# Row scaling and logits of the first expert network kept on chip, its iteration spread out, and the first routing's list product with its operands exchanged

## The chip, the cores and the metric

The kernel runs on one core of a Trainium2 chip. The metric is the device time in microseconds (us) of one execution, as a median of several. The engines are TensorE (PE: matmuls; PEld: its weight loads), VectorE (DVE), ScalarE (ACT), GpSimd (POOL, which here clears buffers and issues indirect DMAs) and SyncE (SP, which issues plain DMAs). Each engine works through its own queue in order.

## The reference

```python
def reference(x, moe, moe2):              # x: 8 x 3072 x 256
    h = real(fft(fft(x, axis=1), axis=2)).reshape(24576, 256)
    # first network: 8 experts, 256 -> 1024 -> 256
    P = exp(h @ moe.w_gate - max)
    for _ in range(8):                    # "scaling"
        P /= P.sum(1) + 1e-9
        P /= P.sum(0) + 1e-9
        P *= N / E
    out = sum(P[:, e:e+1] * (relu(h @ moe.w1[e]) @ moe.w2[e]) for e in range(8))
    # second network: 8 experts, each row goes to its best one
    logits = out @ moe2.w_gate
    e = argmax(logits, axis=1); p = softmax(logits)[e]
    return p * (relu(out @ moe2.w1[e]) @ moe2.w2[e])
```

## The kernel before

The program has five stages: the transform (0 to 195 us), a first routing (195 to 245), the first network (245 to 440), a second routing (436 to 470) and the second network (470 to the end). All but a small part of P is negligible, so the first network, too, computes only chosen rows per expert: three tiles of 128 rows for each of the eight experts, and five overflow tiles f0 to f4, whose rows belong to different experts and whose weights are therefore gathered row by row. P has 29 x 8 = 232 columns on 128 partitions. All matrix products of the networks are done in three passes with each operand split in a high and a low part (`w1h`, `w1l`, `xh`, `xl`, `hh`, `hl`, `w2h`, `w2l`); ACT makes the high parts (L831, L857, L887), DVE the low ones (L837, L427, L436).

**First routing.** DVE forms one-hot factors `ah` (128 wide) and `bv` (58 columns: two values of 29 tiles); 64 small matmuls (L560) add their products to a list `pt` of 128 x 58, from which DVE reads row indices (`hidx`), signs and prices; POOL then gathers the rows of the first tiles (`Xg<-H`), DVE puts them together into `x`, PE transposes them (L854) and the first expert's products (L901) start. Around the list product stand gate products (L1264, halves of 16 matmuls that make w2 times the second gate, so that the second network's logits come with the rows) and empty matmuls on zeros (L1283). `G2` is the string that says how many of each (g and w) stand at each of the stage's points.

**First network.** The order of the work is written by hand. A clock of numbered slots runs through the experts: 0 to 20 in each expert, 0 to 7 the first product, 12 to 20 the second product of its three tiles; (e, i) is slot i of expert e. `STEPS` says at which slots, counted from `SINK`, the 18 half turns of the iteration (scaling) are done: a start, matmuls that add up the columns (L1007), a turn on DVE between them, and an end that writes the row weights `Rwt`. Before the end is reached (`known`), the rows y of finished tiles are kept unscaled in buffers (`keep`); after it they are scaled and written to `acc` in DRAM at one or two per slot (`sink`), and tiles that come later are scaled as they leave PSUM (L1649). `SENDS` says at which slots POOL adds the third tile of each expert to `acc` by an indirect DMA, since its rows also belong to another expert. The gathers of an overflow tile's weights (`fw`, `rawc`, `gd`) stand in the same POOL queue.

**Second routing.** It needs the eight logits of each row, which it reads back from `acc` (`ask`); the rows of third tiles are corrected by one matmul with a one-hot matrix (`arrive`, L1408). Then come the argmax, the positions, and a gather of the second network's rows (`Xg<-acc`, L803). `part("u", 0, i)` splits one of the four weight pieces of the second network's first expert.

Of the kernel before, what the change touches and what calls it, by code (L numbers as in the profile page):

```python
# [7 lines left out]
F32 = mybir.dt.float32  # L8
# [554 lines left out]

def route1(nc, rt, L, rmx, K, R, keep, pool, ring, hooks):
# [109 lines left out]
    o.tt(eq, ja[:, NSL:NSL + 8, None].to_broadcast([128, 8, NSL]), ja[:, None, :NSL].to_broadcast([128, 8, NSL]), ALU.is_equal)  # L674
    o.tt(eq, eq, gp[:, None, :NSL].to_broadcast([128, 8, NSL]), ALU.mult)
    hooks[4]()
# [11 lines left out]
    def signs():  # L688
# [9 lines left out]

        o.red(gq, eq, ALU.add)
# [16 lines left out]
    def targets():  # L716

        lq = S([2, E], name="lq")
# [6 lines left out]
        o.cp(R["l7"], lq[:, :, E - 1])  # L725
# [310 lines left out]
def dense(tc, ctx, A, K, rt, R, Ld, H, Pd, out, wg2):  # L1036
# [69 lines left out]
    with tc.For_i(0, NT, 1) as i:  # L1106
# [17 lines left out]
        for s in range(2):  # L1124
# [27 lines left out]
         ("t", 6, "c"), ("t", 7, "a"), ("w1", 1, "a"), ("w2", 1, "b")]  # L1152
# [5 lines left out]
def run(tc, ctx, A, out, H, acc, Ld, Pd, Gd, Zd):  # L1158
# [19 lines left out]
    for nm, sh, dt in (("gm", [1], F32), ("ovf", [1], F32), ("sel", [max(NF1, NF2), 8], F32), ("hidx", [NT1], I32),  # L1178
                       ("sg", [NT1], F32), ("valid", [NT1], F32), ("prim", [NT1], F32), ("apos", [E], I32), ("oidx", [NF1], I32), ("l7", [2], F32),
# [41 lines left out]
    with tc.manual_schedule():  # L1221
# [27 lines left out]
        with ExitStack() as st:  # L1249
# [7 lines left out]
            def gates2(e, qs=(0, 1)):  # L1257
# [16 lines left out]
                if e < 3 or e == E - 1:  # L1274
                    fetch()
# [24 lines left out]
            with ExitStack() as s1:  # L1300
# [39 lines left out]
                def low(k):  # L1340
                    for f in lows[k]:
                        f()

                signs, later = route1(nc, rt, L, rmx, K, R, S, r1, ring, [fill(i) for i in range(1, 5)] + [lambda: low(0)])
# [20 lines left out]
            with ExitStack() as s1:  # L1365
# [4 lines left out]
                def rest():  # L1370
                    later[2]()
                    sp.close()
                    return P(st, "yb", 15, side="right"), P(s1, "sk", 1, side="right")

                lg = kp.tile([128, NT1, 8], F32, name="lg")

                def ask():
# [7 lines left out]
                turned, more = moe1(nc, K, R, acc, moe, W, part, X, xg, Gd, *rows("w1", "w2"), xb, pt, zeros, zt, later[:2] + (rest, lambda: low(1), grab), ask, rt.C("tro"), lambda i: warm(2), lambda: xg.tile([128, CAP, HW], F32, name="Xg").rearrange("p a b -> p (a b)")[:8, :512])  # L1385
            with ExitStack() as s1:
# [8 lines left out]
                def arrive(choose):  # L1395
                    a, b, n8 = E * CAP - CAP, E * CAP, [128, NT1, 8]
                    hot = xg.tile([128, CAP, HW], F32, name="Xg").rearrange("p a b -> p (a b)")
                    oht, ohr, mv = hot[:, :NT1], hot[:, 32:160], hot[:, 160:160 + 8 * NT1].rearrange("p (t e) -> p t e", e=8)
                    o.ts(oht, rt.C("at"), R["l7"][:, 0:1], ALU.is_equal)
                    o.ts(ohr, rt.C("i128"), R["l7"][:, 1:2], ALU.is_equal)  # L1400
# [4 lines left out]
                    o.tt(mv, oht[:, :, None].to_broadcast(n8), lg[:, a:a + 1].to_broadcast(n8), ALU.mult)  # L1405
                    more(Y2[1])
                    p = pt.tile([128, 512], F32, name="pt")
                    nc.tensor.matmul(p[:, :8 * NT1], ohr, mv.rearrange("p t e -> p (t e)"), start=True, stop=True)  # L1408
# [20 lines left out]
                for i in (2, 3):  # L1429
                    part("u", 0, i, nc.vector)  # L1430
# [404 lines left out]
```

## Time and profile before

| | us |
|---|---|
| timed, median of 3 | 666.21 |
| timed, lowest and highest | 665.62, 670.52 |
| profiled execution, its own time | 660.63 |
| span of the profiled execution | 658.5 |
| PE busy in the span | 624.5 |
| DVE, ACT, POOL busy | 430.6, 327.6, 200.5 |

The profiled execution is 5.58 us shorter than the timed median. Differences are worked out against the profiled execution and then taken off the median. "Busy" counts matmuls that overlap with their neighbours; PEclk is the mean clock granted to TensorE, where 1.00 stands for 2.4 GHz and 0.50 for 1.2 GHz.

### The profile page before, as it was taken

The page shows a single profiled execution, that of the slowest core. Times are in us where ns is not written, and L with a number is a line of the kernel's source. Part 1 is how long each engine was busy: PE and PEld are TensorE (multiplying, and loading weights), DVE is VectorE, ACT ScalarE, POOL GpSimd, SP SyncE. Part 2 cuts the span into 40 slices and gives each one's busy share as a digit, 9 for nine tenths or more (in the row PEclk, how much of TensorE's full clock was granted, in tenths as well). Part 3 has the DMA queues.
Part 4 walks back from the last instruction along what each step waited for, and adds up shares of the span by engine and source line. Part 5 has one row for each costly group of instructions (what it writes and reads, how often), then busy time and mean ns, then how long its engine had stood idle before and what let it go on. Part 6 is the DMA issues. An engine that isn't in the chain of part 4 may idle for free.

```text
span 658.5 us, 12591 instructions
## 1 busy us (share of the span) xinstructions
PE 624.5 (95%) x4776; PEld 601.2 (91%) x4782; DVE 430.6 (65%) x958; ACT 327.6 (50%) x731; POOL 200.5 (30%) x326
## 2 busy tenths in 40 slices
PE   9999999999998999997989898999699999999995
PEld 6899999999998988997989798987599999999995
DVE  4697787778238959759899473657345844844751
ACT  3455545555544404755545773652245644744651
POOL 0002220122010078850101142201486665322342
PEclk9999999999999869998999898999799999999998
DMA  8999999999989865876747897787465367347321
GB/s 220 293 235 298 272 262 285 274 278 305 353 266 347 352 191 172 235 254 201 248 135 231 275 241 264 182 262 246 150 226 190 127 235 299 116 194 272 133 117 36
DMA packets 60142, 152.66 MB, mean 232 GB/s; under 512 B 11651, under 2 KB 29195, under 8 KB 52524
## 3 DMA queue, kind: packets, MB, share of 16 engines
q1 hardware_dynamic: 50716, 114.66, 56.6%
q0 software_dynamic: 8896, 36.64, 16.8%
q8 instruction: 39, 0.64, 0.4%
q10 hardware_dynamic: 464, 0.51, 0.2%
q14 instruction: 27, 0.22, 0.1%
HBM read 101.61 MB, written 50.07 MB: 230 GB/s over the span
## 4 chain that ended last, share of the span: by engine, by line
PE 47%; DMA 10%; DVE 8%; ACT 3%; issue 2%; SPq 0%; POOL 0%; POOLq 0%; DVEq 0%; ACTq 0%
PE py L934 19%; PE ph L901 15%; PE ph L947 5%; PE py L1264 3%; DMA out_dram<-zt 2%; DMA acc<-y 2%; DVE hl L436 2%; DMA rawc<-in_w_dram,Rfrow 2%; DVE w2l L837 2%; PE pt L854 1%; PE py L1283 1%; DMA acc<-zt 1%; DMA Xg<-acc,Rgidx 1%; DVE w1l L837 1%; DMA acc<-y,Rapos 1%
## 5 line engine op out<-in xcount | busy, mean ns | idle before, releaser
L934 PE MATMUL py<-w2h,hh 128*128 128x256 f32 (+1 forms) x472 | 137.3, 291 | 0.0
L436 DVE SCALAR_TENSOR_TENSOR hl<-ph,hh 128x384 fp32r<-128x384 f32 (+1 forms) x161 | 84.7, 542 | 79.0 <-ACT hh L887 78.5
L934 PE MATMUL py<-w2h,hl 128*128 128x256 f32 (+1 forms) x472 | 134.9, 286 | 1.2 <-DVE hl L436 1.2
L934 PE MATMUL py<-w2l,hh 128*128 128x256 f32 (+1 forms) x472 | 134.5, 285 | 0.3 <-DVE w2l L839 0.3
L887 ACT ACTIVATE hh<-ph 128x384 fp32r<-128x384 f32 (+1 forms) x161 | 75.7, 482 | 54.7 <-PE ph L901 34.2
L934 PEld LDWEIGHTS py<-w2h,hl 128*128 128x128 f32 x472 | 90.1, 191 | 2.1 <-DVE hl L436 2.1
L934 PEld LDWEIGHTS py<-w2l,hh 128*128 128x128 f32 x472 | 90.3, 191 | 0.5 <-DVE w2l L839 0.5
L934 PEld LDWEIGHTS py<-w2h,hh 128*128 128x128 f32 x472 | 90.3, 191 | 0.1
L901 PE MATMUL ph<-xh,w1h 128*128 128x384 f32 x256 | 68.5, 348 | 3.5 <-DVE hl L436 3.4
L901 PE MATMUL ph<-xl,w1h 128*128 128x384 f32 x256 | 66.3, 340 | 0.0
L901 PE MATMUL ph<-xh,w1l 128*128 128x384 f32 x256 | 66.2, 340 | 0.0
L808 POOL DMA_INDIRECT out_dram<-y,Rorow x30 | 35.1, 1171 | 81.8 <-ACT hh L887 45.8
L126 POOL TENSOR_TENSOR lc<-hd 128x32 f32<-128x32 f32 (+1 forms) x25 | 9.5, 380 | 165.9 <-ACT hd L122 150.8
L74 PE MATMUL pp<-ca,w 96*128 96x96 f32 x512 | 59.0, 275 | 0.0
L74 PEld LDWEIGHTS pp<-ca,w 96*128 96x128 f32 x512 | 58.2, 192 | 0.5 <-ACT Z L97 0.2
L901 PEld LDWEIGHTS ph<-xh,w1h 128*128 128x128 f32 x256 | 45.5, 190 | 6.5 <-DVE hl L436 5.0
L84 DVE COPY t<-pp 128x512 f32<-128x512 f32 (+2 forms) x56 | 33.3, 608 | 24.7 <-PE pp L82 24.7
L91 PE MATMUL pp<-cb,t 128*128 128x128 f32 x368 | 47.5, 276 | 0.6 <-DVE t L84 0.6
L901 PEld LDWEIGHTS ph<-xl,w1h 128*128 128x128 f32 x256 | 47.0, 190 | 0.1
L901 PEld LDWEIGHTS ph<-xh,w1l 128*128 128x128 f32 x256 | 46.9, 189 | 0.0
L76 ACT ACTIVATE at<-pp 128x384 f32<-128x384 f32 x64 | 31.1, 491 | 30.6 <-PE pp L74 30.0
L91 PEld LDWEIGHTS pp<-cb,t 128*128 128x128 f32 x368 | 44.4, 192 | 0.9 <-DVE t L84 0.8
(340 smaller groups left out, 1249.6 us busy)
## 6 DMA issues: line engine op xcount, KB each, us to landing
out_dram<-zt SPq DMA_DIRECT2D x48, 512.0 KB, 6.9
H<-hd SPq DMA_DIRECT2D x24, 562.0 KB, 10.6
xa<-in_xa_dram SPq DMA_DIRECT2D x32, 384.0 KB, 10.5
xm<-in_xm_dram SPq DMA_DIRECT2D x32, 384.0 KB, 8.5
rawa<-in_w_dram SPq DMA_DIRECT2D x8, 1024.0 KB, 5.1
rawb<-in_w_dram SPq DMA_DIRECT2D x8, 1024.0 KB
rawa<-in_u_dram SPq DMA_DIRECT2D x8, 1024.0 KB, 9.9
rawb<-in_u_dram SPq DMA_DIRECT2D x8, 1024.0 KB
```

What stands on the lines that cost most here:

```text
L74: nc.tensor.matmul(p[:M, i], lhs(4 * h + i), ca, start=True, stop=True)
L76: nc.scalar.activation(out=at[:M, :, :, s0:s0 + 4], in_=p[:M].rearrange("m s g j -> m g j s"), func=AF.Copy)
L84: nc.vector.tensor_copy(out=t[:, :n, :M], in_=p[:, :n, :M])
L91: nc.tensor.matmul(p[:M, i * 128:(i + 1) * 128], t[:, i, :M], cb[:, (g0 + i) * 128:(g0 + i + 1) * 128], start=True, stop=True)
L436: self.nc.vector.scalar_tensor_tensor(out, a, s, b, op0, op1)
L808: nc.gpsimd.indirect_dma_start(out=dst, out_offset=bass.IndirectOffsetOnAxis(ap=idx, axis=0), in_=src, in_offset=None, **kw)
L837: eng.tensor_tensor(out=lv, in0=rv, in1=hv.bitcast(F32), op=ALU.subtract)
L887: self.nc.scalar.activation(out=a[:, :n], in_=p[:, :n], func=AF.Relu)
L901: self.nc.tensor.matmul(p[:, :N], w, xx, start=(i == 0), stop=(i == 5))
L934: self.nc.tensor.matmul(p[:, :nd], c, W[2 + m // 4][w][:, m % 4, :nd], start=(m == 0 and i == 0), stop=(m == 7 and i == 2))
L947: self.nc.tensor.matmul(p[:, m * 128:(m + 1) * 128], w[:, k, (m0 + m) * 128:(m0 + m + 1) * 128], x[:, k, i * 128:(i + 1) * 128], start=(k ...
L1264: nc.tensor.matmul(p[:, i * 96:(i + 1) * 96], raw["t", e][k][:, m * 128:(m + 1) * 128], wg2[:, k], start=(k == 0), stop=(k == 1))
```

## The change

It does four things.

1. In the first routing the list product has its operands exchanged: `bv` (58 columns) is now the stationary operand and `ah` (128 columns) the moving one; the result of 58 x 128 is copied by ACT and transposed back by PE (`turned`). A seventh gate half is done ahead of the counts, eight empty matmuls instead of two stand before the product and two gate halves instead of three behind it. Two operations on `eq` and one low part of w1 move behind the reading of the list. The gate weights of expert 7 come into another buffer.
2. The turns of the scaling are spread from 43 to 64 slots: the start moves from slot (2, 8) to (2, 11), the end from (4, 8) to (5, 8). Three more y buffers lie in an `Xg` tile, and the sends begin in expert 5 instead of 4.
3. The scaling of kept rows moves from ACT to DVE; DVE also copies each tile's eight logits to `lg`, and a one-hot pair for each third tile is made there (`spot`). The two DMAs of `ask` that read the logits back are gone; `arrive` does seven matmuls in place of one.
4. `part("u", 0, 3)`, with the fetch that follows it, moves from before the second routing's gathers to slot (0, 1) of the second network.

```diff
+    def swapped(self, pl, ah, bv, a, n, first, last):
+        nv = bv.shape[1] * bv.shape[2]
+        for i in range(n):
+            self.nc.tensor.matmul(pl[:nv, :128], bv[:, :, :, a + i], ah[:, :, i],
+                                  start=first and i == 0, stop=last and i == n - 1)
+
+    def turned(self, pl, nv, t):
+        self.nc.scalar.activation(out=t[:nv], in_=pl[:nv, :128], func=AF.Copy)
+        p = self.pt.tile([128, 512], F32, name="pt")
+        self.nc.tensor.transpose(p[:, :nv], t[:nv], self.K["ident"][:nv, :nv])
+        return p
...
-        rt.put(pl, ah, bv, a, n, a == NSL, a + n == NSL)
+        rt.swapped(pl, ah, bv, a, n, a == NSL, a + n == NSL)
         a += n
+    hooks[4]()
+    pl = rt.turned(pl, 2 * NT1, T([128], name="lt"))
...
-                if e < 3 or e == E - 1:
+                if e < 4:
                     fetch()
...
-                    for a, b in ((0, E * CAP - CAP), (E * CAP, NT1)):
-                        r = row_tile(a) * 128
-                        nc.sync.dma_start(out=lg[:, a:b], in_=acc[r:r + (b - a) * 128].rearrange("(t p) c -> p t c", p=128)[:, :, D:DG])
...
+                    def add(i):
+                        r, m, _ = hot[i]
+                        nc.tensor.matmul(p[:, :8 * NT1], r, m, start=(i == 0), stop=(i == E - 2))
+
                     more(Y2[0])
+                    for i in range(E - 2):
+                        add(i)
                     pg = turned()
...
-                for i in (2, 3):
-                    part("u", 0, i, nc.vector)
+                part("u", 0, 2, nc.vector)
...
+YB = 15
 SINK = (2, 8)
-STEPS = [0, 1, 6, 6, 11, 11, 16, 16, 21, 21, 26, 26, 31, 31, 36, 36, 41, 42]
-FIRST = 3
-ADDS, SENDS = tuple(range(21)), {4: (15, 20), 5: (4, 9, 14, 19), 6: (13, 17), 7: (2,)}
+STEPS = [3, 4, 10, 10, 17, 17, 23, 24, 32, 32, 39, 39, 48, 48, 55, 55, 62, 63]
+FIRST = 1
+ADDS, SENDS = tuple(range(21)), {5: (14, 19), 6: (3, 8, 12, 16), 7: (1,)}
...
-G2 = ("gg", "", "gggggg", "0lz12g3gg", "ggww", "ggg")
+G2 = ("gg", "", "ggggggg", "0lz12g3gg", "ggwwwwwwww", "gg")
...
             if k is None:
-                nc.scalar.activation(out=y[:, :DG], in_=y[:, :DG], func=AF.Copy, scale=R["wt"][:, t:t + 1])
+                o.ts(y[:, :DG], y[:, :DG], R["wt"][:, t:t + 1], ALU.mult)
+            if t // CAP != E - 1:
+                o.cp(lg[:, t], y[:, D:DG])
+                if t < E * CAP and not alone(t):
+                    spot(t // CAP)
+                    hot[-1][2]()
...
+        o.ts(t, rt.C("at"), R["lq"][:, 0, e:e + 1], ALU.is_equal)
+        o.ts(r, rt.C("i128"), R["lq"][:, 1, e:e + 1], ALU.is_equal)
...
+    sl.at(0, 1, lambda: part("u", 0, 3, V))
```

On DVE the place is the end of the scaling. In the kernel before, `Rwt` is the row weights, `xl` and `w1l`, `w2l` the low parts that PE waits for next:

```order
L427 TENSOR_TENSOR pr<-P,Rsel 128x40
L442 TENSOR_REDUCE Rwt<-pr 128x5
L436 SCALAR_TENSOR_TENSOR Rwt<-P 128x24
L427 TENSOR_TENSOR xl<-pt,xh 128x384 x2
L837 TENSOR_TENSOR w1l<-rawa,w1h 128x1024
L837 TENSOR_TENSOR w2l<-rawc,w2h 128x4x256
```

In the changed kernel (where `y` is a tile's rows and `lg` the logits on chip; helper lines stand 13 to 15 further down) the same place reads:

```order
L442 TENSOR_REDUCE Rwt<-pr 128x5
L436 SCALAR_TENSOR_TENSOR Rwt<-P 128x24
L431 TENSOR_SCALAR y<-y,Rwt 128x264
L439 COPY lg<-y 128x8
L431 TENSOR_SCALAR y<-y,Rwt 128x264
L439 COPY lg<-y 128x8
L431 TENSOR_SCALAR y<-y,Rwt 128x264
L439 COPY lg<-y 128x8
L427 TENSOR_TENSOR xl<-pt,xh 128x384 x2
```

Three scalings and their copies now stand between the row weights and `xl`, and more of them between the low parts that follow.

On POOL the place is experts 4 and 5. Before, the additions to `acc` of the third tiles of experts 0 to 3 (by `Rapos`) are mixed with the gathers of overflow tile 4's weights:

```order
L808 DMA acc_58<-y_3445,Rapos_86 1152x265
L808 DMA acc_58<-y_3812,Rapos_86 1536x265
L803 DMA fw_4657<-in_w1_dram,Rfrow_90 128x2048
L808 DMA acc_58<-y_4155,Rapos_86 1920x265
L803 DMA rawc_4716<-in_w2_dram,Rfrow_90 128x2048
L803 DMA gd_4718<-Gd_61,Rfrow_90 128x64
L808 DMA acc_58<-y_4502,Rapos_86 2304x265
```

In the changed kernel:

```order
L816 DMA fw_4629<-in_w1_dram,Rfrow_90 128x2048
L816 DMA rawc_4686<-in_w2_dram,Rfrow_90 128x2048
L816 DMA gd_4688<-Gd_61,Rfrow_90 128x64
L1667 MEMSET y_4835 128x1
L821 DMA acc_58<-y_3461,Rapos_86 1152x265
L821 DMA acc_58<-y_3817,Rapos_86 1536x265
```

All three gathers stand ahead of the first addition to `acc` now; what follows them is the clearing of a column of a y buffer.

## Rows read from the trace of the kernel before

**Rows 1.** What PE waits for from 195 us on: total, times, longest.

```profile
PE pt L1007 <- DVE xl L427: 6.3, 2, 3.8
PE pt L854 <- DMA Xg<-acc,Rgidx: 5.6, 1, 5.6
PE ph L901 <- DVE hl L436: 3.4, 3, 2.6
PE pt L881 <- DVE xl L427: 3.0, 1, 3.0
```

**Rows 2.** Windows, experts 2 to 6: length, busy by engine (PE to POOL), clock, DMA.

```profile
285.60:316.50 30.90, 26.66 (x187) 26.13 (x187) 25.55 (x65) 17.86 (x43) 4.37 (x8) 0.94 0.70 224
316.50:344.40 27.90, 25.39 (x192) 25.18 (x191) 24.76 (x61) 15.13 (x37) 2.94 (x4) 1.00 0.51 169
344.40:375.00 30.60, 27.25 (x192) 26.41 (x191) 22.05 (x51) 20.75 (x50) 4.81 (x5) 0.94 0.78 246
375.00:399.20 24.20, 24.20 (x184) 24.20 (x183) 14.11 (x30) 13.20 (x31) 7.98 (x6) 1.00 0.97 281
399.20:427.90 28.70, 26.08 (x185) 25.76 (x184) 16.82 (x28) 16.43 (x37) 7.68 (x8) 0.94 0.71 199
```

**Rows 3.** The same view, the stretch after the longest of these waits.

```profile
309.20:312.50 3.30, 3.30 (x17) 3.30 (x16) 3.16 (x10) 1.46 (x5) 0.00 (x0) 0.50 0.43 42
```

**Rows 4.** Timeline of DVE in expert 2: start, length, what.

```profile
303.53 0.30 DVE L431 TENSOR_SCALAR P<-P,Rgm 128x232 f32<-128x232 f32 x1
...
307.54 0.56 DVE L442 TENSOR_REDUCE cs<-P 128x8 f32<-128x232 f32 x1
...
310.96 0.16 DVE L433 TENSOR_SCALAR cs<-total 128x8 f32<-128x8 f32 x1
...
313.86 1.21 DVE L837 TENSOR_TENSOR w2l<-rawc,w2h 128x1024 fp32r<-128x1024 f32 x1
```

**Rows 5.** Timelines of ACT, SP, POOL; in brackets idle time before, and its end.

```profile
363.49 2.14 ACT L1657 ACTIVATE y<-y,Rwt 128x264 f32<-128x264 f32 x5 [4.54 <-DVE Rwt L442]
...
401.98 1.06 ACT L831 ACTIVATE w2h<-rawc 128x1024 fp32r<-128x1024 f32 x1 [7.84 <-DMA rawc<-in_w_dram,Rfrow]
...
364.03 0.81 SPq L1669 DMA_DIRECT2D acc<-y  x2
...
366.29 0.10 POOL L1646 MEMSET y<- 128x1 f32 x1 [14.43 <-DMA acc<-y]
...
389.74 1.28 POOL L803 DMA_INDIRECT rawc<-in_w_dram,Rfrow  x1 [0.30 <-issue]
```

**Rows 6.** Timeline of PE in the first routing.

```profile
224.35 0.59 PE L1283 MATMUL py<-zb 128*128 128x512 bf16 x2 [0.36 <-ACT g L1266]
224.99 6.98 PE L560 MATMUL pt<-bv,ah 128*128 128x58 bf16 x64
...
241.92 1.76 PE L560 MATMUL py<-bq,ah 128*128 128x16 bf16 x24
243.53 0.42 PE L854 MATMUL pt<-ident,x 128*128 128x128 f32 x2
...
245.72 0.44 PE L901 MATMUL ph<-xh,w1h 128*128 128x384 f32 x1
```

**Rows 7.** Timeline of DVE there: the last piece of the first tile's rows.

```profile
240.16 0.49 DVE L1602 TENSOR_TENSOR x<-Xg 128x127 f32<-128x127 f32 x2
```

**Rows 8.** The chain that ended last, second routing: start, length, what.

```profile
442.83 0.41 PE pt L1408 x2
...
457.88 1.23 DVE w2l L837
459.33 6.46 DMA Xg<-acc,Rgidx
```

**Rows 9.** Tile Xg in the first routing, 232 to 241 us: its gathers.

```profile
DMA to landing us min/median/max: 2.8/3.0/3.9
```

**Rows 10.** DMA issues, 361 to 400 us: KB each, median us to landing.

```profile
acc<-y SPq DMA_DIRECT2D x5, 132.0 KB, 7.3
```

More of the change, by code (lines that the diff above doesn't have):

```diff
@@ L1342, in low @@
                         f()
-                signs, later = route1(nc, rt, L, rmx, K, R, S, r1, ring, [fill(i) for i in range(1, 5)] + [lambda: low(0)])
+                    lows[k].clear()
+                signs, later = route1(nc, rt, L, rmx, K, R, S, r1, ring, [fill(i) for i in range(1, 5)] + [lambda: lows[0].pop(0)()])
                 X = {}
@@ L1372, in rest @@
                     sp.close()
-                    return P(st, "yb", 15, side="right"), P(s1, "sk", 1, side="right")
+                    return P(st, "yb", YB, side="right"), P(s1, "sk", 1, side="right")
                 lg = kp.tile([128, NT1, 8], F32, name="lg")
+                hot = []
                 def ask():
-                    for a, b in ((0, E * CAP - CAP), (E * CAP, NT1)):
-                        r = row_tile(a) * 128
-                        nc.sync.dma_start(out=lg[:, a:b], in_=acc[r:r + (b - a) * 128].rearrange("(t p) c -> p t c", p=128)[:, :, D:DG])
                     for _ in range(5):
                         zeros(2)
-                turned, more = moe1(nc, K, R, acc, moe, W, part, X, xg, Gd, *rows("w1", "w2"), xb, pt, zeros, zt, later[:2] + (rest, lambda: low(1), grab), ask, rt.C("tro"), lambda i: warm(2), lambda: xg.tile([128, CAP, HW], F32, name="Xg").rearrange("p a b -> p (a b)")[:8, :512])
+                turned, more = moe1(nc, K, R, rt, lg, hot, acc, moe, W, part, X, xg, Gd, *rows("w1", "w2"), xb, pt, zeros, zt, later[:2] + (rest, low, grab), ask, rt.C("tro"), lambda i: warm(2), lambda: xg.tile([128, CAP, HW], F32, name="Xg").rearrange("p a b -> p (a b)")[:8, :512])
             with ExitStack() as s1:
@@ L1404, in arrive @@
                          R["wt"][:, a:b, None].to_broadcast([128, CAP, 8]), ALU.mult)
-                    o.tt(mv, oht[:, :, None].to_broadcast(n8), lg[:, a:a + 1].to_broadcast(n8), ALU.mult)
+                    hot[-1][2]()
                     more(Y2[1])
-                    p = pt.tile([128, 512], F32, name="pt")
-                    nc.tensor.matmul(p[:, :8 * NT1], ohr, mv.rearrange("p t e -> p (t e)"), start=True, stop=True)
+                    add(E - 2)
                     o.tt(lg, lg, p[:, :8 * NT1].rearrange("p (t e) -> p t e", e=8), ALU.add)
@@ L1590, in first, with moe1 @@
         return self.moe.free_first(self.w[f, 0], self.x[f // CAP], f % CAP)
-def moe1(nc, K, R, acc, moe, W, part, X, xg, Gd, w1f, w2f, xb, pt, zeros, zt, rest, ask, trash, warm, grow):
+def moe1(nc, K, R, rt, lg, hot, acc, moe, W, part, X, xg, Gd, w1f, w2f, xb, pt, zeros, zt, rest, ask, trash, warm, grow):
     o = Ops(nc)
@@ L1643, in keep @@
     def keep(t, p):
-        y = late["y"].tile([128, DW], F32, name="y")
+        n = late["n"] = late.get("n", -1) + 1
+        if YB <= n < YB + CAP:
+            if n == YB:
+                late["x"] = xg.tile([128, CAP, HW], F32, name="Xg")
+            y = late["x"][:, n - YB, :DW]
+        else:
+            y = late["y"].tile([128, DW], F32, name="y")
         if t < E * CAP and not alone(t):
@@ L1656, in add @@
             if k is None:
-                nc.scalar.activation(out=y[:, :DG], in_=y[:, :DG], func=AF.Copy, scale=R["wt"][:, t:t + 1])
+                o.ts(y[:, :DG], y[:, :DG], R["wt"][:, t:t + 1], ALU.mult)
[3 more added lines that the diff above has]
+                    spot(t // CAP)
+                    hot[-1][2]()
             if t < E * CAP:
@@ L1677, in send, with spot, moved @@
             scatter(nc, a, i, y, compute_op=ALU.add)
+    def spot(e):
+        if e % 2 or e == E - 1:
+            late["hot"] = xg.tile([128, CAP, HW], F32, name="Xg").rearrange("p a b -> p (a b)")
+        t, r, m = (late["hot"][:, 400 * (1 - e % 2) + a:400 * (1 - e % 2) + b] for a, b in ((0, NT1), (32, 160), (160, 160 + 8 * NT1)))
+        o.ts(t, rt.C("at"), R["lq"][:, 0, e:e + 1], ALU.is_equal)
+        o.ts(r, rt.C("i128"), R["lq"][:, 1, e:e + 1], ALU.is_equal)
+        def moved():
+            n8 = [128, NT1, 8]
+            o.tt(m.rearrange("p (t e) -> p t e", e=8), t[:, :, None].to_broadcast(n8), lg[:, CAP * e:CAP * e + 1].to_broadcast(n8), ALU.mult)
+        hot.append((r, m, moved))
     def begin():
@@ L1687, in moe1 @@
             f()
+    rest[3](0)
     xt = moe.turn(lambda i: x[0][:, i], warm)
-    for i, f in zip((0, 1, 3, 4), (rest[3], rest[0], rest[1], begin)):
+    for i, f in zip((0, 1, 3, 4), (lambda: rest[3](1), rest[0], rest[1], begin)):
         sl.at(0, i, f)
@@ L1733, in moe1 @@
     late["q"] = nc.scalar
+    spot(E - 1)
     def more(n):
```

19 lines of the change are left out of this document (7 added, 12 removed).

## The prediction

> **What bounds the kernel now.** PE is busy for 624.5 of 658.5 us, so the time to be had is where PE waits or runs at half clock. I read first what PE waits for from the first routing on [rows 1]: the scaling's column sums (L1007, 6.3 us in two waits of 3.8 and 2.5), the gather of the second network's rows (5.6), the low part `hl` in the first product (3.4, of which 2.6 in one piece), and the transposes that wait for `xl` (L881, 3.0). Then the windows of experts 2 to 6 [rows 2]. Expert 5 has no wait and takes 24.2 us; the five together take 30.9 + 27.9 + 30.6 + 24.2 + 28.7 = 142.3, which is 21.3 more than five times 24.2. The waits of 3.8, 2.5, 3.0 and 2.6 explain 11.9 of that. After the first of them PE stays busy for 3.3 us with a granted clock of 0.50, 1.2 in place of 2.4 GHz [rows 3]; experts 4 and 6 have the same mean clock of 0.94 as expert 2, while expert 3, whose wait was 2.5 us, has 1.00. Three such stretches of about 3.4 us lose some 1.7 us each, 5.1 in all. So 17.0 us are lost to waits and clock in these experts; the other 4.3 I take for work that differs between them.
>
> **The change part by part.** *Scaling, start and turns.* The start and the first half turn hold DVE from 303.53 to 308.10, 4.6 us, and a later turn from 310.96 to 313.86, 2.9 us [rows 4]. In expert 2 DVE is busy for 25.55 us, in expert 3 for 24.76 [rows 2], both more than the 24.2 in which PE could be done: DVE is the bound there, and the turns are its surplus. Spread from 43 to 64 slots, a pair of turns comes every 7 or 8 slots and not every 5; a slot is 24.2 / 21 = 1.15 us. Expert 2 gives up about one turn (25.55 - 2.9 = 22.7), expert 3 as well (21.9); both then fit under 24.2. The start keeps its 4.6 us and its first product one slot later. I count two slots, 2.3 us, as what PE has in hand, and keep a wait of 2.5 us out of 3.8; for all other turns in experts 2 to 4 I keep 1 us out of the second wait of 2.5.
>
> *Scaling, the end and the scaled rows.* At the end ACT stood idle for 4.54 us until `Rwt` was there and then scaled five tiles in 2.14 us, while what makes `xh` and so `xl` queued behind it [rows 5]: this is the wait of 3.0. Now DVE scales. The nearest price is a DVE operation on 232 columns, 0.30 [rows 4]; with 264 columns and a copy of eight logits I take 0.45 per tile (an estimate from that row; ACT's 2.14 / 5 = 0.43 for the scaling alone would make it 0.6), and 0.7 for a one-hot pair with its product (three operations of 0.2 to 0.3). What is late next is twofold. `xl` now stands behind three scalings and copies on DVE, 1.35 us. And ACT's next kept row needs a y buffer that is freed only when a write to `acc` has landed: before, a write issued at 364.03 released POOL at 366.29, 2.3 us later [rows 5]. With the end of the turn (1.4) and two scalings ahead of it, ACT is blocked for some 4.5 us, and queued behind it are the high parts of the next tile; most of that PE covers with the 24 matmuls of a tile, and I keep 1.2 us of the wait of 3.0. Over expert 5 as a whole DVE gets 14.1 (its own work) + 4.4 (one and a half turns) + 13 x 0.45 = 5.9 + 3 x 0.7 = 2.1, together 26.5 against 24.2: 2.3 us too much, a wait that was not there. Expert 6 comes to 16.8 + 5 = 22 and fits; I put 0.5 there.
>
> *The gathers of overflow tile 4.* In expert 6 ACT waited 7.84 us for `rawc`, whose gather POOL issued only at 389.74, behind additions to `acc` that wait for writes [rows 5]; PE's wait of 2.6 for `hl` and the half clock after it (1.7) follow from that. Now the three gathers stand ahead of all additions, and the additions queue behind them, which nobody in expert 5 or 6 waits for. I take these 4.3 us as gained.
>
> So of the 17.0 us lost there remain 2.5 + 1 + 1.2 + 2.3 + 0.5, and 1 for a half-clock stretch that still occurs: 8.5. **Gain 8.5**, between 17.0 (no wait left) and about 0 (DVE's new work makes as many waits as go).
>
> *The list product.* 64 matmuls take 6.98 us, 109 ns each; the product with 16 moving columns runs at 1.76 / 24 = 73 ns [rows 6]. If the time follows the moving columns, (109 - 73) / 42 = 0.86 ns a column, 128 columns give 169 ns and 10.8 us; if the 73 ns are the floor and the moving columns don't count, 4.7 us. The count of instructions is unchanged and no row shows 58 stationary columns, so I take the 109 ns as they are, between both ends. Six more empty matmuls at 0.3 each, less a little that was spent waiting anyway, start it 1.1 us later; the copy by ACT and the transpose back add 0.9. The list, complete at 224.99 + 6.98 = 231.97, would so be complete at 233.97. From there to the end of the first rows' last piece it was 240.65 - 231.97 = 8.68 us [rows 7], which gives 242.65; PE, which came to the transposes at 243.53 because gate products were in front, now has a half less behind the list and reaches them before that. With 245.72 - 243.53 = 2.2 us from there to the first product [rows 6] it starts at 244.85, **0.9 us earlier**; with 169 ns it is 2.9 later, with 73 ns 3.2 earlier. The two operations on `eq` and the low part of w1 (1.2 like that of w2 [rows 4]) move behind the reading, where DVE waits for the gather; if that didn't hide them they would cost some 2 us, inside these ends. The seventh gate half ahead of the counts is moved, not added: PE waits for DVE there, and without that wait it costs ahead of the list what it saves behind it.
>
> On this product the Trainium skill speaks on both sides. "TensorE: Matmul & The Clock Gate", section "Weight-path perf modes — Fast Weight Load (FWL) and DoubleRow", says that weights are read fast only when there are 128 of them, which 58 stationary columns would give up; its section "Back-to-back issue gap" has 81 ns for a matmul with 128 moving columns, by which the product would be 5.2 us and this term about 2.7. The trace agrees with neither yet, since its 109 ns stand at 58 moving columns.
>
> *The second routing.* `arrive` gets six more matmuls of the kind that takes 0.41 [rows 8], 2.5 us; they stand ahead of the logits' transposes, on the chain. The two loads of `ask` were issued early on SP and are on no path; that they go brings nothing. **Loss 2.5.**
>
> *The weight piece.* The gather of the rows starts at 459.33, 0.2 us after the low part of that piece ends (1.23 from 457.88) [rows 8]; without it, it could start 1.2 us earlier. It then takes 6.46 us to land, while the same gather in the first routing takes 2.8 to 3.9 [rows 9]; the 1 MB fetch, which is issued when the piece's raw buffer comes free, runs in that time and moves away with it. That is 1.2 at least and 1.2 + 3.7 = 4.9 at most; since the last writes to `acc` must also land first, I take the middle, **gain 3.1**. The piece itself (1.06 on ACT, 1.23 on DVE) goes into the second network's first expert, where I count it as hidden: expert 5's row of the windows shows 10 us to spare on DVE in an expert without turns [rows 2]; uncovered it would cost 2.3.
>
> Against the second half of that term the Trainium skill has a rule: "DMA: Bandwidth & Descriptors", section "Queues, rings and completion order", has the DMA engines change between the queues with each packet, so that a fetch would not hold a gather back until it is done. By that rule the term would be nearer 1.2 than 3.1. The 6.46 us against 3.0 speak for a fetch that does hold it back, but they do not show which of the two rows is the exception.
>
> Sum: 8.5 + 0.9 - 2.5 + 3.1 = 10.0. The profiled execution took 660.6, 5.6 less than the median; 650.6 there, and **656.2** for a median of 666.2.
>
> **The rivals.** *All waits go.* The turns fit, the end hides behind PE's tile, and nothing new is late: 17.0 + 0.9 - 2.5 + 3.1 = 18.5, so 647.7. For it: expert 5's 24.2 us shows that PE can run through. Against it: the start's 4.6 us are unchanged, and ACT's wait for a buffer is new.
>
> *DVE takes it back.* If a scaled tile costs 0.6 and the scalings, which stand in front of `hl` and the low parts of weights, make PE wait in experts 5 and 6 as the turns did in 2 and 3 (3.7 to 6.7 us over 24.2 in each), 7 us more are lost: 3.0 are left, so 663.2. For it: 26.5 against 24.2 on DVE even at my price. Against it: the surplus is in one expert, and the tiles that come later are still scaled by ACT.
>
> *Slower: ACT waits for buffers.* If the writes that free y buffers take 7.3 us, as others did in that stretch [rows 10], and not 2.3, each of expert 5's three kept tiles holds ACT 5.0 us longer, and the high parts `hh` with it. That is 15 us and three half-clock stretches of 1.7, 20.1 together: 10.1 slower, so 676.3. It turns the sign from a landing time of 2.3 + 10.0 / 3 = 5.6 us on. For it: DMA was at a share of 0.97 in expert 5 before. Against it: the removed loads and later sends thin that out, and the first write came in 2.3.
>
> That the change doesn't do what it says is possible for the list product alone: at 169 ns the sum is 10.0 - 3.8 = 6.2 and the time 660.0, within the forecast's own width.
>
> **How the numbers follow.** A difference of under 1% (6.7 us) can hardly be told from none here. Forecast 0.51 (own range 650 to 661), all waits go 0.17, DVE takes it back 0.24, ACT waits for buffers 0.08. Faster than 659.5: 0.46 of the first, 0.17, and 0.04 of the third, 0.67. Slower than 672.9: 0.06 of the last. The rest, 0.27, is within 1%. The range leaves out most of the last case and the far ends of the others: 644 to 667.
>
> **What would show it.** In the changed kernel's profile: experts 2 to 4 near 27, 25 and 26 us; PE's wait for L1007 once and near 2.5 us; no wait of PE for `hl` in expert 6, and the gather of `rawc` issued in expert 5 without a write in front; expert 5 longer than 24.2, with DVE busy over 90% of it. The list product near 7 us and the first L901 after it about a microsecond earlier; L1408's six more matmuls as 2.5 us; the gather landing about 3 us after its issue. The prediction is wrong if ACT's rows in expert 5 show idle time that ends with a write to `acc`, or if the waits of experts 2 and 3 stay although the turns are apart, which would mean that the burst and not the density makes them.

## The result, and the profile after

The changed kernel is slower: a median of 669.36 us against 666.53 of the kernel before, ratio 1.0058 (95% interval 1.0033 to 1.0083). On another chip it was 1.0044 (1.0018 to 1.0071). The forecast was 656.2, faster by 10.

The profiled execution took 667.02 us, its span is 665.2, 6.7 longer than before. Stage by stage, from the start of the first matmul of each stage in the traces (us; "changed, again" is a second profiled execution of the same kernel, "product put back" the run *put_again* below):

| stage | before | changed | changed, again | product put back |
|---|---|---|---|---|
| transform | 195.2 | 197.8 | 197.7 | 199.5 |
| first routing, to the list product | 29.8 | 32.5 | 32.8 | 33.0 |
| list product | 7.0 | 14.8 | 14.8 | 6.9 |
| from there to the first expert's first product | 13.8 | 15.2 | 10.4 | 10.5 |
| experts 0 and 1 | 39.8 | 41.5 | 39.9 | 39.8 |
| experts 2 to 6 | 142.3 | 132.1 | 136.1 | 133.0 |
| expert 7 and second routing | 42.5 | 42.5 | 45.4 | 45.4 |
| second network | 188.2 | 188.7 | 187.1 | 188.5 |

The transform is not touched by the change. Its 2.5 us are a stretch at half clock from 46 us on, which the profiled execution of before happened not to have; all others had it, one built on the kernel before (*price*) among them. The same five microseconds in the two traces, before and changed (length, busy PE, PEld, DVE, ACT, POOL, clock, DMA share, GB/s):

```profile
46.00:51.00 5.00, 5.00 (x46) 5.00 (x45) 4.93 (x8) 2.94 (x7) 0.86 (x2) 1.00 0.82 218
```

```profile
46.00:51.00 5.00, 5.00 (x26) 5.00 (x26) 3.87 (x7) 1.72 (x4) 0.00 (x0) 0.51 1.03 245
```

This may also be part of why that execution was 5.6 us under its median. What is left, 3 to 4 us, agrees with the ratio. It is a sum of large parts: 7 to 12 us lost in the first routing, 6 to 10 gained in experts 2 to 6, and nothing gained, or 3 lost, in the second routing.

In the first routing, PE's timeline of the changed kernel, to be set beside [rows 6]:

```profile
226.92 3.48 PE L1296 MATMUL py<-zb 128*128 128x512 bf16 x8 [1.98 <-ACT g L1279]
230.33 14.84 PE L567 MATMUL pt<-ah,bv 128*58 128x128 bf16 x64
245.52 0.35 PE L573 MATMUL pt<-ident,lt 58*128 58x58 f32 x1 [0.36 <-ACT lt L571]
...
258.56 1.01 PE L1296 MATMUL py<-zb 128*128 128x512 bf16 x2 [3.99 <-remote]
...
260.37 1.04 PE L914 MATMUL ph<-xh,w1h 128*128 128x384 f32 x2
```

64 matmuls take 14.84 us, 232 ns each, where 6.98 stood before. The windows of the two parts of that product show that it is not the clock: 16 matmuls in 3.50 us at a clock of 0.99 are 219 ns each, and the other 48, in 11.26 us at 0.50, are 235. The clock halves, and a matmul takes hardly longer.

```profile
230.40:233.90 3.50, 3.50 (x16) 2.87 (x17) 1.04 (x1) 0.00 (x0) 0.00 (x0) 0.99 0.73 274
233.90:245.20 11.30, 11.26 (x50) 8.61 (x48) 0.00 (x0) 0.00 (x1) 0.00 (x0) 0.50 0.00 0
```

The first product of the first expert (L914) is 14.65 us later than before. Of that, 2.6 come from the transform; 2.7 from the eight empty matmuls, which begin with PE idle for 1.98 us behind ACT and then run at half clock (3.48 us); 7.9 from the product; 0.7 from copy and transpose; and 4.0 from a stop of PE at 254.57, ended by nothing that the profile can name ("remote"). Gate products at the higher clock and one half less of them give some 3 us back.

In experts 2 to 6 the waits of [rows 1] are gone. What PE waits for after, from 195 us on:

```profile
PE py L1296 <- remote: 4.0, 1, 4.0
PE ph L914 <- DVE hl L436: 3.9, 5, 1.7
...
PE pt L867 <- DMA Xg<-acc,Rgidx: 1.9, 1, 1.9
PE py L947 <- ACT y L1670: 1.4, 1, 1.4
...
PE pt L1020 <- DVE cs L442: 0.6, 1, 0.6
```

The scaling's column sums (now L1020) cost 0.6 in place of 6.3, the transposes behind `xl` don't appear with a wait of their own, and the longest wait for `hl` is 1.7; it lies in expert 6, where DVE is busy for 24.2 of 26.2 us. In expert 5 ACT stands idle for 5.98 us, until a write to `acc` has landed and a y buffer is free, and the next matmul of PE on `py` starts at 401.69 after the wait of 1.4 above:

```profile
401.07 0.20 ACT L1669 ACTIVATE y<-Row 128x1 f32<-128x1 f32 x1 [5.98 <-DMA acc<-y]
```

The windows of the five experts, to be set beside [rows 2], have a clock of 1.00 in every one:

```profile
301.80:327.80 26.00, 24.96 (x186) 24.46 (x186) 20.84 (x54) 17.74 (x42) 2.95 (x4) 1.00 0.63 207
327.80:354.00 26.20, 25.20 (x190) 24.76 (x189) 23.39 (x54) 15.01 (x36) 3.96 (x4) 1.00 0.70 225
354.00:380.50 26.50, 25.76 (x193) 25.18 (x192) 24.38 (x57) 15.21 (x36) 2.93 (x4) 1.00 0.78 262
380.50:407.70 27.20, 25.24 (x189) 24.71 (x188) 20.99 (x61) 15.63 (x38) 2.93 (x4) 1.00 0.60 204
407.70:433.90 26.20, 24.52 (x183) 24.20 (x183) 24.21 (x70) 14.19 (x30) 4.75 (x3) 1.00 0.86 241
```

POOL's timeline shows the gather of `rawc` at 385.72 with nothing in front of it (389.74 before, [rows 5]), and then the new queue of additions to `acc`, the first at 413.42, the last at 464.49, behind which the gather of the second network's rows starts, although the list that it needs has been complete on PE since 462.36 + 3.31 = 465.67:

```profile
385.72 0.94 POOL L816 DMA_INDIRECT rawc<-in_w_dram,Rfrow  x1 [0.30 <-issue]
...
413.42 1.62 POOL L821 DMA_INDIRECT acc<-y,Rapos  x1 [11.52 <-DVE y L431]
...
464.49 1.56 POOL L821 DMA_INDIRECT acc<-y,Rapos  x1 [2.95 <-ACT w2h L844]
469.26 1.01 POOL L816 DMA_INDIRECT Xg<-acc,Rgidx  x1 [3.21 <-DMA acc<-y,Rapos]
```

```profile
462.36 3.31 PE L560 MATMUL pt<-bv,Xg 128*128 128x60 bf16 x29
```

Before, the gather started behind a weight piece on DVE and took 6.46 us to land [rows 8]. In the chain that ended last it now takes 2.91, but it starts behind an addition to `acc`:

```profile
464.49 3.91 DMA acc<-y,Rapos
...
469.26 2.91 DMA Xg<-acc,Rgidx
```

The six more matmuls of `arrive` are there, 12 records because each f32 matmul here leaves two:

```profile
447.14 2.51 PE L1413 MATMUL pt<-Xg 128*128 128x232 f32 x12
```

### The profile page after: what moved, and what is told of

It reads as the page before. It is cut to its first block, busy times and chain, and to the rows that moved or that the text cites. A ratio compares the mean times of both kernels' runs of the same rounds, so it can differ in the third digit from the quotient of the medians.

```text
span 665.2 us, 12673 instructions
## 1 busy us (share of the span) xinstructions
PE 636.6 (96%) x4801; PEld 605.8 (91%) x4801; DVE 441.9 (66%) x1019; ACT 321.7 (48%) x718; POOL 195.5 (29%) x325
## 5 line engine op out<-in xcount | busy, mean ns | idle before, releaser
L914 PE MATMUL ph<-xh,w1h 128*128 128x384 f32 x256 | 68.0, 347 | 4.3 <-DVE hl L436 3.9
L914 PE MATMUL ph<-xl,w1h 128*128 128x384 f32 x256 | 65.3, 336 | 0.0
L914 PE MATMUL ph<-xh,w1l 128*128 128x384 f32 x256 | 65.3, 336 | 0.0
L74 PE MATMUL pp<-ca,w 96*128 96x96 f32 x512 | 60.8, 280 | 0.4 <-DVE w L160 0.4
L74 PEld LDWEIGHTS pp<-ca,w 96*128 96x128 f32 x512 | 59.8, 196 | 1.0 <-issue 0.5
L821 POOL DMA_INDIRECT out_dram<-y,Rorow x30 | 33.4, 1114 | 83.8 <-ACT hh L900 36.8
L914 PEld LDWEIGHTS ph<-xh,w1h 128*128 128x128 f32 x256 | 45.0, 189 | 7.6 <-DVE hl L436 6.0
L914 PEld LDWEIGHTS ph<-xh,w1l 128*128 128x128 f32 x256 | 46.4, 188 | 0.0
L914 PEld LDWEIGHTS ph<-xl,w1h 128*128 128x128 f32 x256 | 46.3, 188 | 0.0
L151 DVE TENSOR_TENSOR xa<-xa,xm 96x1024 f32<-96x1024 f32 x32 | 38.9, 1214 | 11.1 <-DMA xm<-in_xm_dram 11.1
```

The source lines that it names most:

```text
L74: nc.tensor.matmul(p[:M, i], lhs(4 * h + i), ca, start=True, stop=True)
L151: e.tensor_tensor(out=xa[:, c], in0=xa[:, c], in1=xm[:, c], op=ALU.add)
L821: nc.gpsimd.indirect_dma_start(out=dst, out_offset=bass.IndirectOffsetOnAxis(ap=idx, axis=0), in_=src, in_offset=None, **kw)
L914: self.nc.tensor.matmul(p[:, :N], w, xx, start=(i == 0), stop=(i == 5))
```

## The experiments

The theory after these rows: the list product is what makes the change slower, because a moving column whose elements don't lie next to each other takes 1.8 ns whatever the clock (S). Rivals: the 58 stationary columns are slow (W), the clock (K), or the stop and the gate halves around the product (G). For the rest: the spread of the turns makes the gain in experts 2 to 6 (D, against A: taking the scaling off ACT), and the second routing takes back what the late additions cost (Q). All runs below that have "product put back" carry the other parts of the change.

**price.** Eight groups of 24 matmuls behind the product of the kernel before, with eight empty ones ahead of each:

```diff
+    warm8()
+    for i in range(24):
+        nc.tensor.matmul(pd[:, :58], ahs(i), bvs(i), start=True, stop=True)
+    warm8()
+    for i in range(24):
+        nc.tensor.matmul(pd[:58, :128], bvs(i), ahs(i), start=True, stop=True)
...
+    warm8()
+    for i in range(24):
+        nc.tensor.matmul(pd[:, :128], tb1[:, :128], tb1[:, 128:], start=True, stop=True)
```

> The kernel before with eight extra groups of 24 bf16 matmuls behind its list product, eight empty matmuls ahead of each; the groups' results are not used. Theory S (the moving operand's spacing): a moving column whose elements lie 40 to 48 bytes apart takes about 1.8 ns at either clock, so 58 of them 105 ns and 128 of them 227, and what is stationary doesn't matter. Then, ns per matmul: (1) ah still, bv moving 58: 107; (2) bv still, ah moving 128: 227; (3) bv still, a dense 128 moving: under 110; (4) dense 58 still, ah moving 128: 227; (5) dense 128 still, ah moving: 227; (6) dense 58 still, dense 128 moving: under 90; (7) ah still, dense 58 moving: under 80; (8) dense 128 still, dense 128 moving: under 90. Theory W (the 58 stationary columns): (2), (3), (4) and (6) are all slow, 200 or more, and (5) is near 110. Theory K (the half clock alone): (2) under 130 while the empty matmuls hold the clock at 1.00, double behind that.

PE's timeline, groups (1) to (8) in order; `trib` is the dense operand:

```profile
238.20 2.74 PE L683 MATMUL pt<-bv,ah 128*128 128x58 bf16 x24
...
244.04 5.67 PE L686 MATMUL pt<-ah,bv 128*58 128x128 bf16 x24
...
253.17 2.66 PE L689 MATMUL pt<-trib,bv 128*58 128x128 bf16 x24
...
257.59 5.55 PE L692 MATMUL pt<-ah,trib 128*58 128x128 bf16 x24
...
266.46 5.57 PE L695 MATMUL pt<-ah,trib 128*128 128x128 bf16 x24
...
274.95 1.52 PE L698 MATMUL pt<-trib 128*58 128x128 bf16 x24
...
278.14 1.80 PE L701 MATMUL pt<-trib,ah 128*128 128x58 bf16 x24
...
281.50 1.50 PE L704 MATMUL pt<-trib 128*128 128x128 bf16 x24
```

Length by 24: 114, 236, 111, 231, 232, 63, 75 and 62 ns (with the last matmul's tail, some 7 ns of each). The moving operand decides: `ah` moving costs 231 to 236 with `bv`, 58 dense or 128 dense columns standing still; a dense moving operand costs 62 and 63 at the same sizes beside a dense one that stands still. Groups (6) to (8) ran at a clock of 1.00, the others wholly or in part at 0.50, but (2) is as slow as the product above at either. W falls with (6), K with the windows above. Against what S said, the stationary operand matters too when it is spaced: (3) against (6) is 111 against 63, (7) against (8) 75 against 62. That 75 is near the 73 ns of the product with 16 moving columns and `ah` still [rows 6], which so looks like a floor and not like a point on a line.

**put_back, route_back, dense.** The product alone put back; the whole of part 1 undone; the exchanged operands kept, but `ah` written densely:

```diff
-        rt.swapped(pl, ah, bv, a, n, a == NSL, a + n == NSL)
+        rt.put(pl, ah, bv, a, n, a == NSL, a + n == NSL)
...
-    pl = rt.turned(pl, 2 * NT1, T([128], name="lt"))
```

```diff
+        m = self.K["irx"].shape[2]
+        ah = pool(128 * m)[:, :128 * n].rearrange("p (i r) -> p i r", r=128)
+        self.o.tt(ah, self.C("i128")[:, None, :].to_broadcast([128, n, 128]), rb[:, a:a + n, None].to_broadcast([128, n, 128]), ALU.is_equal)
+        return ah.rearrange("p i r -> p r i")
...
-        ah = rt.rows(ring, rb, a, n)
+        ah = rt.lines(ring, rb, a, n)
...
```

> The changed kernel with the list product's operands put back (ah still, bv moving, no copy and no transpose back); everything else of the change stays. Theory P (the loss is the product's): the product takes 7 us again and not 14.8, the first product of the first expert starts some 8.6 us earlier after the transform, and the time is 0.98 to 0.99 of before. Rival G (the loss is the wait of 4 us and the order of the gate halves around it): the time stays at or above before.

> The changed kernel with the whole of part 1 undone: operands, gate halves, empty matmuls, the low parts of w1, the buffer of expert 7's gate weights. Parts 2 to 4 stay. What they gain by the trace of after is 10.3 us in experts 2 to 6 and nothing from there to the second network: 0.983 to 0.988 of before. If the empty matmuls and the early gate half cost nothing of their own, this equals the run with the product alone put back; if they cost the 3 us by which the product started late, this is 3 us (0.5%) faster than that one.

> The changed kernel, with ah written so that the 128 elements of each moving column group lie next to each other; the operands stay exchanged. DVE makes ah from other operands and may be slower at it. Theory S: a matmul falls from 227 ns to under 110, or to DVE's pace if DVE needs longer for ah (4.56 us for three pieces before); the time is 4 to 8 us under that of the changed kernel. Theory W: a matmul stays near 227 ns and the time at 1.006 of before or above.

Ratios to before on one chip: 0.9881 (0.9852 to 0.9909), 0.9888 (0.9842 to 0.9934) and 0.9893 (0.9863 to 0.9922). All three beat the kernel before, and by these ratios the changed one, by some 10 us; for dense, 4 to 8 had been expected. P holds against G: put_back has the stop too, and a longer one, and still gains. In its trace:

```profile
231.91 6.94 PE L560 MATMUL pt<-bv,ah 128*128 128x58 bf16 x64
...
251.51 1.01 PE L1295 MATMUL py<-zb 128*128 128x512 bf16 x2 [4.71 <-remote]
```

And in the trace of dense, with the operands still exchanged, 105 ns a matmul, W out once more. The clock is 1.00 all through the product there, so half clock is not what makes `bv` standing still dearer than a dense operand:

```profile
230.67 6.72 PE L573 MATMUL pt<-ah,bv 128*58 128x128 bf16 x64
```

route_back does not come out 0.5% under put_back, though the intervals are as wide as that. From the transform to the first product it is 50.4 us in put_again and 50.6 before, in the table above: what the late start behind the empty matmuls costs, the rest of part 1 gives back behind the product. (route_back's own trace has 54.3 there, with three waits of PE of 1.9 us together that the profile doesn't explain, and half clock behind them; that is open.)

**after_again, put_again.** The changed kernel and put_back once more, on one other chip, unchanged.

> The changed kernel as it is, on the chip of this call. By the stages of its first trace: product 14.8 us again; 7 to 9 us above the run with the product put back if the stop of 4 us comes in both or in neither.

> The run with the product alone put back once more, on the chip of this call. Theory P: 1 to 1.5% below before, as the first time. In its trace the wait of PE for the last addition and the gather in the second routing, and the stop of 4 us at the first transposes, come again if the kernel makes them; if the stop is absent, it belongs to single executions.

1.0044 (1.0018 to 1.0071) and 0.9935 (0.9900 to 0.9969): 0.9% or 8.8 us apart on the same chip, as expected. put_again is 0.65% below before, less than the 1 to 1.5% expected. The product took 14.83 us again. The stop came in neither; in after_again PE goes through the same place without a wait:

```profile
254.28 0.38 PE L867 MATMUL pt<-ident,x 128*128 128x128 f32 x2
254.49 0.59 PE L1296 MATMUL py<-zb 128*128 128x512 bf16 x2
```

So the change does not make it: the same kernels run with it and without (dense had one of 2.95 us; steps_back, steps_old_sends_new, act_scales, part_back and between had none). put_back and dense, which had it, ran on one chip, the runs just named without it on two others, so that chip and single execution can't be told apart. Nothing in these traces names its cause, and it stays open. In after_again the experts give 6.2 us and not 10.2, because of a wait for `hl` of 3.9 us in expert 2 with half clock behind it; other executions have that wait at 1.6 to 1.9 or not at all; that is open, too.

**steps_back, steps_old_sends_new.** Put_back with the scaling's slots as before; the second keeps the later sends:

```diff
-STEPS = [3, 4, 10, 10, 17, 17, 23, 24, 32, 32, 39, 39, 48, 48, 55, 55, 62, 63]
-FIRST = 1
+STEPS = [0, 1, 6, 6, 11, 11, 16, 16, 21, 21, 26, 26, 31, 31, 36, 36, 41, 42]
+FIRST = 3
...
-ADDS, SENDS = tuple(range(21)), {5: (14, 19), 6: (3, 8, 12, 16), 7: (1,)}
+ADDS, SENDS = tuple(range(21)), {4: (15, 20), 5: (4, 9, 14, 19), 6: (13, 17), 7: (2,)}
```

> The run with the product alone put back, and in addition the slots of the scaling as before: start at (2, 8), 43 slots, end at (4, 8), and the sends as before. DVE still scales the rows and keeps the logits. Theory D (the spread makes the gain in experts 2 to 6): PE's waits for L1020 and for the transposes come back, and the gather of rawc is late again; 7 to 10 us slower than with the product alone put back, ratio to before 0.998 to 1.003. Rival A (taking the scaling off ACT makes the gain): at most 3 us slower, ratio under 0.993.

> The same, but with the sends of the changed kernel, so that the gathers of overflow tile 4's weights stand ahead of the additions to acc. If the gather's lateness was worth 4.3 us, this is 3 to 5 us faster than the run with the old slots and the old sends, and PE's wait of 2.6 us for hl in expert 6 is gone; if the wait came from the scalings alone, the two are equal.

0.9967 (0.9932 to 1.0002) and 0.9969 (0.9931 to 1.0007). The stage shows more than the total. Experts 2 to 6 in put_back, in steps_back and in steps_old_sends_new, one window each:

```profile
293.94:425.92 131.98, 125.51 (x933) 123.14 (x931) 113.64 (x292) 77.79 (x182) 19.02 (x23) 1.00 0.73 231
```

```profile
287.77:430.33 142.56, 130.39 (x932) 128.61 (x931) 114.49 (x289) 78.26 (x182) 30.66 (x35) 0.95 0.73 224
```

```profile
289.45:428.15 138.70, 129.39 (x932) 127.78 (x931) 114.13 (x289) 78.83 (x182) 23.57 (x28) 0.96 0.73 226
```

D holds: with the old slots and the old sends all 10.6 us come back, and with them, in steps_back, PE's waits:

```profile
PE pt L1019 <- DVE xl L427: 6.3, 2, 3.8
...
PE pt L893 <- DVE xl L427: 2.3, 1, 2.3
```

The two runs with the old slots differ by 142.6 - 138.7 = 3.9, but that is not the sends' part: they differ from expert 4 on, and 2.3 of the 3.9 lie in experts 2 and 3. In expert 6, where the late gather was to cost 4.3, it is 25.96 against 24.19 us, 1.8; PE's wait for `hl` there, 1.5 in steps_back, is gone with the new sends. The ratios of the two runs show no difference.

But in the second routing, from expert 7's first product to the second network's, steps_back takes 39.8 us, put_back 45.6 and put_again 45.4. So 5.6 to 5.8 of the 10.6, a bit over half of what spread and sends gain, are given back there, and steps_back is that much less behind in the ratio. The sends alone do not do this: steps_old_sends_new has the changed kernel's sends and takes 40.8. With the old slots its additions begin 24.5 us ahead of expert 7's first product, with the spread, whose scaling ends a whole expert later, 20.1 to 20.5; its gather starts 34.4 us behind that product, that of put_back and put_again 38.2.

steps_back also shows the moved weight piece where no addition stands in the way. Its gather starts 1.0 us behind the list (before: 2.0) and lands after 3.6 us (before: 6.46 [rows 8]):

```profile
463.05 1.75 POOL L815 DMA_INDIRECT Xg<-acc,Rgidx  x1 [11.12 <-DVE Rgidx L427]
```

```profile
Xg<-acc,Rgidx POOLq DMA_INDIRECT x1, 3.6
```

**act_scales.** Put_back, with the kept rows scaled on ACT again:

```diff
-                o.ts(y[:, :DG], y[:, :DG], R["wt"][:, t:t + 1], ALU.mult)
+                nc.scalar.activation(out=y[:, :DG], in_=y[:, :DG], func=AF.Copy, scale=R["wt"][:, t:t + 1])
```

> The run with the product alone put back, but ACT scales the kept rows again; DVE still copies the logits. If DVE's load is a bound in experts 5 and 6 (26.5 against 24.2 us by the prediction), this is 1 to 3 us faster; if ACT's queue is what the scalings hurt, 1 to 4 us slower, with PE's wait for the transposes behind xl back near 3 us.

0.9932 (0.9901 to 0.9963); experts 2 to 6 take 132.69 us against 132.0 and 133.0:

```profile
287.73:420.42 132.69, 125.53 (x932) 123.29 (x931) 107.75 (x273) 84.38 (x198) 23.06 (x29) 1.00 0.75 234
```

Neither of the two expectations: where the rows are scaled makes no difference in these experts that this shows, once the turns are apart. A falls.

**part_back.** Put_back, with the weight piece ahead of the gathers again:

```diff
-                part("u", 0, 2, nc.vector)
+                for i in (2, 3):
+                    part("u", 0, i, nc.vector)
...
-    sl.at(0, 1, lambda: part("u", 0, 3, V))
```

> The run with the product alone put back, and in addition the weight piece of the second network split ahead of the gathers again, as before. Theory: the gather waits again for the low part and lands late behind the fetch, 2 to 4 us slower than with the product alone put back. Rival (the third tiles' last addition to acc sets the gather's start, and the skill's rule that queues take turns holds): under 1 us of difference.

0.9948 (0.9914 to 0.9983). From expert 7 to the second network 48.3 us against 45.4 and 45.6, 2.7 to 2.9 longer, and PE's wait for the gather is 9.5 us, 4.7 in put_back:

```profile
PE pt L866 <- DMA Xg<-acc,Rgidx: 9.5, 1, 9.5
```

The piece costs here about what it was forecast, 3.1, but not in the way that was expected. Its low parts end at 451.48 + 2.35 = 453.83, long before the gather, and the gather itself lands in 2.8 us. What is late is the last addition to `acc`: beside the fetch of 1 MB, issued at 453.86, it takes 7.6 us to land, where the same addition takes 4.1 in put_again, and the gather starts behind it.

```profile
451.48 2.35 DVE L849 TENSOR_TENSOR w2l<-rawb,w2h 128x1024 fp32r<-128x1024 f32 x2
452.02 2.12 POOL L820 DMA_INDIRECT acc<-y,Rapos  x1 [2.96 <-issue]
453.86 0.34 SPq L1230 DMA_DIRECT2D rawb<-in_u_dram  x1
460.45 1.02 POOL L815 DMA_INDIRECT Xg<-acc,Rgidx  x1 [6.32 <-issue]
```

```profile
acc<-y,Rapos POOLq DMA_INDIRECT x1, 7.6
```

So it is the fetch and not the piece on DVE. The rule of the Trainium skill ("DMA: Bandwidth & Descriptors", section "Queues, rings and completion order"), by which the fetch would not hold the gather back until it is done, gave 1.2. In this trace both queues move packets between 455 and 459 us, as the rule has it, and the addition still lands some 3.5 us later than without the fetch; the measurement decides for the larger number.

**between.** Put_back with 53 slots, the end at (4, 19) and the additions from (5, 8) on:

```diff
-STEPS = [3, 4, 10, 10, 17, 17, 23, 24, 32, 32, 39, 39, 48, 48, 55, 55, 62, 63]
-FIRST = 1
-ADDS, SENDS = tuple(range(21)), {5: (14, 19), 6: (3, 8, 12, 16), 7: (1,)}
+STEPS = [3, 4, 9, 9, 15, 15, 21, 21, 28, 28, 34, 34, 40, 40, 46, 46, 52, 53]
+FIRST = 3
+ADDS, SENDS = tuple(range(21)), {5: (8, 12, 17), 6: (1, 5, 10, 15), 7: (1,)}
```

> The product put back, the scaling's slots between the two kernels (53 slots from (2, 11), end at (4, 19)), and the additions of the third tiles sent from (5, 8) on, right behind the gathers of overflow tile 4's weights. Theory Q (what experts 2 to 6 gain is taken back in the second routing, because the additions start late and queue behind each other in POOL): experts 2 to 6 stay near 133 us, the gather of the second network's rows starts 3 to 6 us earlier after expert 7's first product than in the run with the product alone put back, and the time is 3 to 6 us below that run. Rival (the additions are held by the bulk transfers, whenever they start): the gather starts no earlier, same time.

0.9878 (0.9804 to 0.9951), a miss for Q as it was put: 46.0 us in the second routing, no less than put_again, and the gather starts 38.2 us behind expert 7's first product, as it does there. That is what the rival said of the gather; the time can't be told from put_again's. Experts 2 to 6 took 134.2. POOL's timeline says why the gather is no earlier:

```profile
386.77 1.76 POOL L820 DMA_INDIRECT acc<-y,Rapos  x1 [8.56 <-DMA acc<-y]
...
397.32 2.79 POOL L820 DMA_INDIRECT acc<-y,Rapos  x1 [8.78 <-DVE Xg L431]
...
453.85 1.89 POOL L820 DMA_INDIRECT acc<-y,Rapos  x1 [3.26 <-issue]
458.88 1.01 POOL L815 DMA_INDIRECT Xg<-acc,Rgidx  x1 [3.13 <-issue]
```

Nine additions run one behind the other from 386.77 to the gather, 8.0 us each; the changed kernel's eight took (469.26 - 413.42) / 8 = 7.0. Each starts only when the one before has landed: the first, issued at 386.77, lands at 396.49, and the next starts at 397.32. The chain started earlier, but had one link more and slower ones. Before, the chain of nine started at 372.12, the eighth had landed by 434, and the last, at 445.56, waited for its data and not for the chain. That the chain, not the list, now sets the gather's start is shown by the rows; an earlier start alone did not mend it. What slows the links is open: beside one fetch a link took 7.6 us instead of 4.1 (part_back), so the rival may be right on the cause as well.

## Why the prediction was wrong

1. **The list product, wrong by its size and sign: this is the failed step.** I took "the 109 ns as they are" and gave 0.9 us of gain, with 169 ns and 2.9 us of loss as the far end. It is 232 ns. I had looked for the danger in the 58 stationary columns, which, dense, cost nothing (63 ns against 62 with 128); it was in the moving operand, whose spaced elements take 1.8 ns a column. The far end was wrong because I drew a line through 73 ns at 16 columns and 109 at 58. The 73 is near the 75 that a spaced `ah` costs when it stands still, a floor; above it the time goes with the columns, 109 / 58 = 1.9 ns each, and 128 of them make 240 ns and 15.4 us. That number could be had from the row that I quoted, by proportion. Without the stop, the first routing lost 58.0 - 50.6 = 7.4 us, with it 11.9.
2. **The start behind eight empty matmuls** was to cost 1.1 and cost about 3, since PE, early by the moved gate half, waited 1.98 us for ACT and then ran them at half clock. The gate products behind gave it back; part 1 without the exchange comes to nothing that a run here shows.
3. **The scaling, right in its sum, in part by luck.** 8.5 forecast, 10.2 and 6.2 in the two executions, 9.3 in put_again. The start's wait was 0.6 and not 2.5, and the buffer wait on ACT 1.4 as against 1.2. DVE's surplus in expert 5 did not show: it was busy for 21.0 us of 27.2, not 26.5 of 24.2; expert 6 had 24.2, for which I had said 22. The gathers of overflow tile 4 were to give 4.3 and no wait for `hl` in expert 6; the wait is 1.7 there, expert 6 took 26.2 us instead of 28.7, and the experiment on the sends gives 1.8. So the start was better than forecast and expert 6 worse. The sign of being wrong that I had named did come, ACT idle in expert 5 until a write to `acc`; it cost PE the 1.4, and is not what made the forecast wrong.
4. **The additions, a step left out.** I wrote that they queue behind the gathers, "which nobody in expert 5 or 6 waits for". True there; but the second routing's gather waits for the last of them. It started 3.6 us after the list's end (469.26 against 465.67) where before it was 2.0, and 6.5 in after_again and put_again. Of the moved weight piece's term, the half on the landing came in full (2.9 instead of 6.46 us); the half on the start, 1.2 earlier, became 1.6 to 4.5 later. With the 2.5 for `arrive`, nothing is left: 42.5 and 45.4 us against 42.5. That the additions come so late is the work of the spread's late end more than of the sends (40.8 us in steps_old_sends_new).
5. **The six matmuls of `arrive`, right** in their length: 2.51 us for 2.5. No run takes them out alone.

With what the table shows, behind the transform, the two executions of the changed kernel sum up to -11.9 - 1.7 + 10.2 + 0.0 - 0.5 = -3.9 and -7.4 - 0.1 + 6.2 - 2.9 + 1.1 = -3.1 (first routing, experts 0 and 1, experts 2 to 6, second routing, second network): 3 to 4 us slower, as measured.

Of the rivals, "slower: ACT waits for buffers" had the sign, but not the mechanism: ACT's wait for a buffer cost PE 1.4 us. "DVE takes it back" is to be seen at most in the 1.7 us for `hl` in expert 6.

## What to carry to other kernels

Before the operands of a small matmul are exchanged, look at how far apart the elements of the operand that will move lie: a price taken from the old moving operand goes by columns and not by instructions, and a point at a floor must not be put on that line. Where a chain of dependent DMAs is moved to a later start, count its links times their landing time against whoever needs the last one, also stages further on; an earlier start of the chain did not bring its end forward (between). Here the change without the exchange, at 0.988 to 0.994 of before, was the better kernel.

## What the runs showed of the hardware that I had not expected

A bf16 moving operand whose elements lie 48 bytes apart (`ah`; 32 in the last 16 matmuls of the product) takes 1.7 to 1.8 ns per column, at a clock of 0.99 as at 0.50 (219 and 235 ns for 128 columns); the dense one is at 62 ns for 128 columns altogether. The Trainium skill ("TensorE: Matmul & The Clock Gate", section "Back-to-back issue gap") has 81 ns for 128 moving columns; the dense groups here are under that, the spaced ones near three times as much. Spaced stationary operands cost, too, but less: 111 ns against 63 with 58 columns, 75 against 62 with 128; whether that comes of the spacing, which differs between the two, or of the count, no run here parts.

An indirect addition to `acc` landed in 4.1 us in put_again and in 7.6 us in part_back, beside a fetch of 1 MB.
